# Gated linear attention with a multiplicative FFN on Trainium2: in three early steps the product of q, k and decays moves behind the masks and to the next chunk

## The chip, the cores and the metric

The kernel runs on one core of a Trainium2 chip. The metric is the device time in microseconds (us) of one execution. Below, PE is TensorE (its weight loads are listed as PEld), DVE is VectorE, ACT is ScalarE, POOL is GpSimd, and SP is SyncE, which here only issues DMAs.

## The reference

For 4 batches of 8 heads with 768 positions and a head size of 48, a state of 48 x 48 per head is decayed and added to at each position, and read by the query:

```python
for t in range(S):
    state = alpha[:, :, t, :, None] * state + np.einsum('bhd,bhe->bhde', k[:, :, t], v[:, :, t])
    y[:, :, t] = np.einsum('bhd,bhde->bhe', q[:, :, t], state)
...
a = x @ w1
b = x @ w2
h = a * b @ w3
return (h @ w_out).astype(np.float32)
```

Here x is the attention's output with the heads side by side, 3072 x 384; w1 and w2 are 384 x 1024, w3 is 1024 x 1024 and w_out 1024 x 384. All weights of the FFN come as 64-bit floats, and the attention's inputs as 32-bit floats.

## The kernel before

**Chunks and steps.** Each batch's 768 positions are cut into 6 chunks of 128, so there are N = 24 chunks. The main loop `for n in range(N + 1)` works on several chunks in each of its turns, here called step n: it ends the attention of chunk n-1, makes the scores of chunk n, and prepares the chunks after them. Steps 0 to 5 (n < FIRST = 6) are the early ones, in which the gate weights are also converted. The fourth to sixth step are n=3, 4 and 5.

**One chunk's work.** `load_kq` (L151, L152), `load_a` (L141 for pairs of chunks, L145 for single ones) and `load_v` (L157) issue the loads. `logs` takes the logarithm of alpha on ACT (L316 for a pair, L324 for one chunk). `decays` sums the logarithms along positions with a triangular matmul (L340 for a pair's chunk, L343 or L346 for others) and ACT makes the exponentials of minus and plus the sum (L349, L350) in the tile e. `decayed` multiplies k and q by them on DVE (L359, tile qk). `transposed` turns qk on PE against the identity (L381), and ACT copies the result from two PSUM banks to the tile qkT (L383, two copies). `scores` multiplies q and k on PE (L454; from chunk 8 on L430), and DVE masks the upper triangle with a bitwise and (L457, two instructions; L440 later). `attend_state` multiplies q with the state T (L474), `attend` the masked scores with v (L485; L482 later), and ACT copies the sum to the tile x (L489), which `store` writes to a DRAM tensor xd (L305, SP). `outer` makes the state's next term from qk and v (L393), and DVE adds it to T (L401, L403); a batch's last chunk, n=5, 11 and so on, has no outer product. At every second chunk `advance` multiplies the state with the decays over the chunk on POOL (L410 to L412); these are gathered through DRAM, with small DMAs on POOL's queue (L331, L352, L354 out, L367 back).

**Buffers.** The tile kq has 3 buffers, so the load for chunk n+3 waits until the product of chunk n has read its own. The tile e has 2, qk has 3, qkT 2, the masked scores ms 2, and v 4. All PSUM results use one ring of 8 banks in the order in which the code asks for them.

**Weights.** `to_fp32` converts a 64-bit weight tile in generator steps that `convert` runs: SP loads it raw (L236, 512 KB; up to 4 in flight), ACT converts the low words (L244) and DVE the mantissa (L245) and the exponent (L248); ACT scales the exponent (L249), DVE puts the number together (L251, L252, L253). `load_gates` then splits it: ACT makes the high part (L260), DVE the low one (L262). `third` makes the third part with two matmuls (L276, L277) and a copy on ACT (L278).

**From step 6 on.** `split_early` splits the attention's output, loaded back from xd (L512), into three parts on ACT (L521) and DVE (L522, and L524 twice). From step 7 on pieces of the two gate products (`gate`, matmuls at L554) are run between the attention's parts, the first of them behind the transposes of step 7. After the last chunk come the remaining gate products, the folding of w3 and w_out into one matrix, and the final product, nearly all of it matmuls at L554.

**What sets the order.** The program's own order and its marks set priorities: `after_marks(...)` opens a context in which what is issued stands behind the marked instructions, and a scheduler then orders each engine's queue. Every engine works through its queue in order. SP's DMAs use 8 semaphores in turn, so a DMA waits until the one eight places ahead of it has landed.

Of the kernel before, what the change touches and what calls it, by code (L numbers as in the profile page):

```python
# [48 lines left out]
def kernel(  # L49
# [18 lines left out]
    N = B * NCH  # L68
# [35 lines left out]
    def bank():  # L104
        return ps.tile([C, 512], FP32, tag="bank", name="bank")
# [3 lines left out]
    def after_marks(*names):  # L109
        stack = ExitStack()  # L110
        for x in names:
            stack.enter_context(tc.issue_after(mark[x]))
        return stack
# [22 lines left out]
    def load_a(n):  # L136
        if paired(n):
            if n % 2 == 0:
                b, c = divmod(n, NCH)
                x = pairs[n // 2 % 2]  # L140
                nc.sync.dma_start(out=x.rearrange("p h s d -> p h (s d)"), in_=alpha[b, :, ds(c * C, 2 * C), :].rearrange("h (p s) d -> p h (s d)", s=2))  # L141
                st["a", n] = st["a", n + 1] = x
        elif n < N:
            st["a", n] = inp.tile([C, H, D], FP32, tag="ac", name="ac", bufs=2)
            nc.sync.dma_start(out=st["a", n], in_=rows(alpha, n))  # L145

    def load_kq(n):
        if n >= N:
            return
        st["kq", n] = inp.tile([C, 2, H, D], FP32, tag="kq", name="kq")  # L150
        nc.sync.dma_start(out=st["kq", n][:, 0], in_=rows(k, n))  # L151
        nc.sync.dma_start(out=st["kq", n][:, 1], in_=rows(q, n))  # L152

    def load_v(n):
        if n < N:
            st["v", n] = vs[n % len(vs)]
            (nc.gpsimd if 2 < n < 8 else nc.sync).dma_start(out=st["v", n][:, :, 0:D], in_=rows(v, n))  # L157
# [122 lines left out]
    def fetch(ahead=3):  # L280
        while weights and len(begun) < ahead:
            begun.append(weights.popleft())
            next(begun[-1])

    def convert(steps, ahead=3):

        for _ in range(steps):
            fetch(ahead)
            if not begun:
                return  # L290
            x = begun.popleft()
            try:
                next(x)
                begun.appendleft(x)
            except StopIteration:
                pass
# [4 lines left out]
    def store():  # L301

        while later:
            dst, src = later.popleft()
            nc.sync.dma_start(out=dst, in_=src)  # L305
# [51 lines left out]
    def decayed(n):  # L357
        if n < N:
            mark["qk", n] = nc.vector.tensor_mul(qks[n % 3][:, :, :, 0:D], st.pop(("kq", n)),  # L359
                                 st.pop(("e", n)).rearrange("p i (h d) -> p i h d", h=H)).ins  # L360
# [9 lines left out]
    def transposed(n):  # L370
        if n >= N:
            return
        qk = qks[n % 3]
        qkT = work.tile([C, 2, NP, C], FP32, tag="qkT", name="qkT")

        tp = [bank().rearrange("p (i j c) -> p i j c", i=2, j=NP) for _ in range(2)]
        for i in range(2):
            for j in range(NP):
                for half in range(2):
                    s = ds(DP * half, DP)  # L380
                    nc.tensor.transpose(tp[half][:, i, j, :], qk[s, i, 2 * j:2 * j + 2, :], ident[s, s])  # L381
        for half in range(2):
            mark["qkT", n] = nc.scalar.copy(qkT[:, :, :, ds(DP * half, DP)], tp[half]).ins  # L383
        st["qkT", n] = qkT
# [116 lines left out]
    def load_early(e):  # L501

        first, chunks = EARLY[e]
        if chunks == 3:
            pieces = ((xb[0][:, XB - KM * TG:].bitcast(FP32), 3),)
        else:
            pieces = ((inp.tile([C, 2, H, D], FP32, tag="kq", name="kq").rearrange("p i h d -> p (i h d)"), 2),
                      *((inp.tile([C, H, D], FP32, tag="ac", name="ac", bufs=2).rearrange("p h d -> p (h d)"), 1) for _ in range(2)))
        st["xT", e], at = [], 0
        for x, width in pieces:  # L510
            x = x.rearrange("p (k t) -> p k t", k=KM)
            nc.sync.dma_start(out=x, in_=x_of(first + at, width))  # L512
            st["xT", e].append((x, ds(at * C, width * C)))
            at += width
# [176 lines left out]
    def run(pieces):  # L691

        for _ in range(pieces):
            if not fill:
                return
            try:
                next(fill[0])
            except StopIteration:
                fill.popleft()
# [20 lines left out]


    FIRST = 6
    begin = {FIRST - 3 + 4 * g: (g, range(FH if g < 4 else KF)) for g in range(5)}
    loads = {8: 1, 11: 2, 15: 3, 20: 4}

    for n in range(N + 1):
        if not 1 < n < FIRST:
            store()
        if n in loads:
            load_early(loads[n])  # L730
        if n != 1 and not 2 < n <= FIRST:
            load_a(n + 5)
        raws = (3, 3, 3, 3, 2, 2, 3, 3)[n] if n < 8 else 4
        for m in (n + 3,) * (n <= FIRST) + (n + 4,) * (n >= FIRST):
            load_kq(m)
            if 2 < n <= FIRST and m == n + 3:
                load_a(n + 5)
            if 1 < n < FIRST:
                store()
            if n < FIRST - 2:  # L740
                fetch(raws)
        if n >= FIRST:
            load_v(n + 2)
        if n:
            attend_state(n - 1)
        if n < N:
            scores(n)
        else:
            for j in range(NP):
                for i in range(2):  # L750
                    attend_low(n - 1, j % 2, i, i ^ (j < 2))
        transposed(n + 1)
        if n == 1:
            decays(3)
            load_a(6)
            with after_marks(("e", 3)):
                logs(4)
        if n == FIRST + 1:
            run(2)
        if n < FIRST:  # L760
            with after_marks("pool"):
                load_v(n + 2)
        if n - 2 in begin and n > FIRST:
            g, tiles = begin[n - 2]
            with after_marks(("ms", n), ("qkT", n + 1)):
                split_early(g)
            fill.extend(gate(g, f) for f in tiles)
        if n == FIRST:
            with after_marks("l", ("qkT", n + 1)):
                split_early(0)  # L770
            fill.extend(gate(0, f) for f in begin[n - 3][1])
        pieces = ((3, 3, 2, 0) if n > FIRST + 3 else (0, 3, 3, 0))[(n - FIRST) % 4] if n >= FIRST else 0
        if n == 0:
            with after_marks(("qkT", 0)):
                logs(2)
            decays(2)
            with after_marks(("e", 2)):
                logs(3)
        early, ready = n < FIRST, len(thirds) if n > 2 else n // 2
        marks = (*[("qkT", n + 1)] * (n < N - 1), *[("qk", n + 1), ("ms", n)] * early, *["x3"] * (n - 2 in begin and n > FIRST))  # L780
        if n < N - 2 and n != FIRST:
            with after_marks(*marks):
                convert(2 if early else 1, raws)
        advance(n)
        turn_v(n)
        if n:
            attend(n - 1)
        outer(n)
        if n > FIRST:
            third(ready)  # L790
        run(pieces > 0)
        if early:
            with after_marks(*marks):
                convert(1, raws)
        with after_marks(*[("ms", n)] * (n < 3)):
            decayed(n + 2)
        if not early:
            with after_marks(*[("qkT", n + 1)] * (n < N - 4)):
                logs(n + 4)
        if n == 4:  # L800
            load_early(0)
        convert(early and n > 0, raws)
        run(pieces > 1)
        if n:
            decays(n + 3)
        if n <= FIRST:
            third(ready)
        if 0 < n < FIRST:
            with after_marks(("e", n + 3)):
                logs(n + 4)  # L810
        if n == FIRST:
            with after_marks("x3", ("e", n + 3)):
                convert(2, raws)
        elif n < N - 2:
            convert(n == FIRST - 1 if early else n % 3 == 0, raws)
        if n == FIRST - 1:
            assert len(done) == 2 * KM
        run(pieces > 2)
        if n == N - 3:
            while begun:  # L820
                convert(1)
            weights.extend(load_out(j) for j in range(KF))
            fetch(4)
# [92 lines left out]
```

## Time and profile before

| what | value |
|---|---|
| three runs | 463.62, 464.98 and 462.82 us; median 463.62 |
| the profiled execution | 462.58 us, with a span of 460.8 us from first to last instruction |
| PE busy | 444.3 us (96%) |
| DVE, ACT, POOL busy | 370.1 us (80%), 270.3 us (59%), 85.7 us (19%) |
| PE busy in 20 to 30, 30 to 40, 40 to 50, 50 to 60 us | 8.56, 8.35, 8.59, 9.45 us |
| PE busy in 60 to 80 us | 20.00 us |
| start of the scores (L454) in n=3, 4, 5, 6 | 29.94, 37.07, 44.66, 50.15 us |
| start of the first gate product (L554) | 58.07 us |
| DMA: bytes in all, mean rate | 79.95 MB, 173 GB/s |

Times count from the start of the span. The timeline lists for one engine the start, the length and the name of each instruction, with equal ones merged (x16), and in brackets how long the engine was idle before it and what ended the wait. The list of waits sums these. The DMA view gives for a transfer the time from its issue to its landing. The granted clock of TensorE is 1.00 of full speed in every stretch.

### The profile page before, as it was taken

Reading aid. Unit: us, or ns where it says so; the run is one execution under the profiler, and the core shown is the slowest. Engines: PE = TensorE matmul, PEld = TensorE weight load, DVE = VectorE, ACT = ScalarE, POOL = GpSimd, SP = SyncE. Lnnn points to the kernel's source line nnn. Section 1 sums busy time; section 2 is a strip of 40 time slices with the busy share of each in tenths; the row PEclk is TensorE's granted clock in tenths of the full one; section 3 lists DMA queues with packets and bytes.
Section 4 is the critical chain, followed back from the end, with each engine's and each line's share of the span. In section 5 each row is a group of like instructions: output and inputs, shape, how many; then the busy total and the mean of one; then the engine's idle time right before and its main releaser. Section 6 shows DMA issues by size and latency. Waiting matters only on the chain.

```text
span 460.8 us, 10652 instructions
## 1 busy us (share of the span) xinstructions
PE 444.3 (96%) x4080; PEld 393.4 (85%) x4080; DVE 370.1 (80%) x600; ACT 270.3 (59%) x507; POOL 85.7 (19%) x171
## 2 busy tenths in 40 slices
PE   4987999999999999999999999999999999999996
PEld 2665699898998988888888888888888999999996
DVE  2869997999989989798999899999537566776671
ACT  4775875758668653777975757566436333343430
POOL 6324232315314240012021010100000000000000
PEclk9999999999999999999999999999999999999999
DMA  9999999999998974445966364521119655665511
GB/s 177 259 206 218 266 221 201 243 214 212 188 233 181 242 179 156 155 112 161 301 198 211 116 172 133 177 68 46 48 51 282 203 151 167 187 186 162 155 53 51
DMA packets 149379, 79.95 MB, mean 173 GB/s; under 512 B 97184, under 2 KB 138784, under 8 KB 149328
## 3 DMA queue, kind: packets, MB, share of 16 engines
q1 hardware_dynamic: 143840, 64.84, 57.4%
q0 software_dynamic: 5488, 14.43, 10.5%
q8 instruction: 32, 0.52, 0.5%
q14 instruction: 19, 0.16, 0.1%
HBM read 57.19 MB, written 22.06 MB: 172 GB/s over the span
## 4 chain that ended last, share of the span: by engine, by line
PE 89%; DMA 4%; SPq 2%; DVE 2%; ACT 2%; issue 1%; DVEq 0%; ACTq 0%
PE bank L554 73%; PE bank L430 3%; PE bank L381 3%; PE bank L482 2%; PE bank L474 2%; DMA x<-in_alpha_dram 2%; PE bank L393 1%; DMA kq<-in_q_dram 1%; PE bank L346 1%; PE bank L419 1%; PE bank L343 1%; SPq L305 1%; SPq L145 1%; PE bank L454 1%; PE bank L485 1%
## 5 line engine op out<-in xcount | busy, mean ns | idle before, releaser
L554 PE MATMUL bank<-x,w 128*128 128x512 f32 (+1 forms) x688 | 163.0, 374 | 0.9 <-ACT qkT L383 0.9
L554 PEld LDWEIGHTS bank<-x,w 128*128 128x128 f32 x688 | 124.6, 188 | 21.1 <-ACT qkT L383 1.2
L554 PE MATMUL bank<-w3o,ab 128*128 128x384 f32 x576 | 100.2, 336 | 0.0
L554 PEld LDWEIGHTS bank<-w3o,ab 128*128 128x128 f32 x576 | 99.9, 188 | 0.2
L554 PE MATMUL bank<-x3b,w 128*128 128x512 f32 (+1 forms) x248 | 71.9, 385 | 0.0
L579 ACT ACTIVATE bank<-bank 128x512 f32<-128x512 f32 (+1 forms) x72 | 41.1, 573 | 34.2 <-PE bank L554 34.2
L554 PEld LDWEIGHTS bank<-x3b,w 128*128 128x128 f32 x248 | 46.4, 188 | 8.4
L628 POOL DMA_DIRECT2D abd<-r x33 | 19.3, 584 | 138.0 <-DVE r L614 116.2
L678 DVE TENSOR_TENSOR ab<-abl,ab 128x1024 fp32r<-128x1024 f32 x24 | 29.4, 1224 | 14.4 <-ACT ab L677 14.4
L383 ACT COPY qkT<-bank 128x512 f32<-128x512 f32 x48 | 26.2, 599 | 22.7 <-PE bank L381 22.7
L563 ACT ACTIVATE t<-bank 128x384 f32<-128x384 f32 x24 | 11.8, 493 | 45.9 <-PE bank L554 45.9
L677 ACT ACTIVATE ab<-abl 128x1024 fp32r<-128x1024 f32 x24 | 25.5, 1062 | 22.1 <-PE bank L554 19.8
L554 PE MATMUL bank<-wo,w3T 128*128 128x384 f32 x192 | 36.3, 337 | 0.0
L249 ACT ACTIVATE power<-power,rebias 128x512 uint32<-128x512 uint32 (+1 forms) x36 | 25.3, 702 | 17.2 <-DVE power L248 16.9
L554 PEld LDWEIGHTS bank<-wo,w3T 128*128 128x128 f32 x192 | 34.1, 188 | 1.2
L565 DVE SCALAR_TENSOR_TENSOR o<-bank,t 128x384 f32<-128x384 f32 x24 | 13.4, 558 | 25.9 <-issue 14.3
L359 DVE TENSOR_TENSOR qk<-kq,e 128x768 f32<-128x768 f32 x24 | 22.9, 954 | 13.8 <-ACT e L350 7.8
L614 DVE TENSOR_TENSOR r<-bank,r 128x512 f32<-128x512 f32 x32 | 21.8, 682 | 9.2 <-PE bank L554 7.7
L679 DVE SCALAR_TENSOR_TENSOR ab<-ab,abl 128x1024 fp32r<-128x1024 f32 x24 | 29.2, 1218 | 0.0
L565 DVE SCALAR_TENSOR_TENSOR r<-bank,r 128x384 f32<-128x384 f32 (+1 forms) x40 | 22.8, 576 | 7.4 <-ACT r L563 6.0
L563 ACT ACTIVATE r<-bank 128x384 f32<-128x384 f32 (+1 forms) x40 | 20.8, 526 | 13.1 <-PE bank L554 10.2
L251 DVE SCALAR_TENSOR_TENSOR mant<-mant,raw 128x512 f32<-128x512 uint32 (+1 forms) x36 | 23.4, 650 | 2.2 <-ACT raw L244 2.2
(115 smaller groups left out, 736.9 us busy)
## 6 DMA issues: line engine op xcount, KB each, us to landing
abl<-abd SPq DMA_DIRECT2D x24, 512.0 KB, 4.3
abd<-r POOLq DMA_DIRECT2D x33, 256.0 KB, 3.3
raw<-in_moe_w_dram SPq DMA_DIRECT2D x64, 128.0 KB, 4.0
raw<-in_moe_w_dram SPq DMA_DIRECT2D x12, 512.0 KB, 5.6
kq<-in_k_dram SPq DMA_DIRECT2D x24, 192.0 KB, 5.0
kq<-in_q_dram SPq DMA_DIRECT2D x24, 192.0 KB, 5.5
xd<-x SPq DMA_DIRECT2D x48, 96.0 KB, 4.0
xT<-xd POOLq DMA_DIRECT2D x6, 768.0 KB, 5.4
```

The source lines that it names most:

```text
L249: nc.scalar.activation(power, power, AF.Relu, scale=2.0 ** 23, bias=rebias)
L251: nc.vector.scalar_tensor_tensor(mant, top, 2.0 ** -20, rest, op0=ALU.mult, op1=ALU.add)
L359: mark["qk", n] = nc.vector.tensor_mul(qks[n % 3][:, :, :, 0:D], st.pop(("kq", n)), st.pop(("e", n)).rearrange("p i (h d) -> p i h d", h=H ...
L383: mark["qkT", n] = nc.scalar.copy(qkT[:, :, :, ds(DP * half, DP)], tp[half]).ins
L554: nc.tensor.matmul(p, w[part][i], x[part][i], start=start and part == parts[0] and i == 0, stop=stop and part == parts[-1] and i == n - 1, ...
L563: nc.scalar.activation(t, p1, AF.Copy, scale=(1.0 + 1.0 / P) * scale)
L565: nc.vector.scalar_tensor_tensor(to, p2, scale, t, op0=ALU.mult, op1=ALU.add)
L579: nc.scalar.activation(p, p, AF.Copy, scale=1.0 + 1.0 / P)
L614: nc.vector.tensor_mul(r[0], p, r[0])
L677: nc.scalar.activation(t[:, 0], ab, AF.Copy, scale=1.0 - 2.0 ** -13)
L678: nc.vector.tensor_sub(t[:, 1], ab, t[:, 0].bitcast(FP32))
L679: nc.vector.scalar_tensor_tensor(t[:, 2], t[:, 0].bitcast(FP32), -1.0 - 1.0 / P, ab, op0=ALU.mult, op1=ALU.add)
```

## The change

A tuple SHORT names the steps 3, 4 and 5. In these, `transposed(n + 1)` is no longer called behind the scores but behind the attention's product and `outer`; ahead of it stands `decayed(n + 1)`, the product of q, k and decays of the next chunk, behind the mark of this step's masks. Before, step n made the product of chunk n+2 and used one that the step before had made. The steps 2, 3 and 4 therefore no longer make the product of chunk n+2, and step 5 makes two, that of chunk 6 and, at its old place, that of chunk 7. The weights' conversion, three generator steps at these places, is divided differently: one behind the masks and two behind the product, in place of two and one behind the marks of qkT, qk and ms. The tiles, the buffers and the instructions' number and size stay.

```diff
--- before.py
+++ after.py
@@ -720,6 +720,7 @@
 
 
     FIRST = 6
+    SHORT = (3, 4, 5)
     begin = {FIRST - 3 + 4 * g: (g, range(FH if g < 4 else KF)) for g in range(5)}
     loads = {8: 1, 11: 2, 15: 3, 20: 4}
 
@@ -749,7 +750,8 @@
             for j in range(NP):
                 for i in range(2):
                     attend_low(n - 1, j % 2, i, i ^ (j < 2))
-        transposed(n + 1)
+        if n not in SHORT:
+            transposed(n + 1)
         if n == 1:
             decays(3)
             load_a(6)
@@ -777,8 +779,11 @@
             with after_marks(("e", 2)):
                 logs(3)
         early, ready = n < FIRST, len(thirds) if n > 2 else n // 2
-        marks = (*[("qkT", n + 1)] * (n < N - 1), *[("qk", n + 1), ("ms", n)] * early, *["x3"] * (n - 2 in begin and n > FIRST))
-        if n < N - 2 and n != FIRST:
+        marks = () if n in SHORT else (*[("qkT", n + 1)] * (n < N - 1), *[("qk", n + 1), ("ms", n)] * early, *["x3"] * (n - 2 in begin and n > FIRST))
+        if n in SHORT:
+            with after_marks(("ms", n)):
+                convert(1, raws)
+        elif n < N - 2 and n != FIRST:
             with after_marks(*marks):
                 convert(2 if early else 1, raws)
         advance(n)
@@ -789,11 +794,18 @@
         if n > FIRST:
             third(ready)
         run(pieces > 0)
-        if early:
+        if n in SHORT:
+            with after_marks(("ms", n)):
+                decayed(n + 1)
+            transposed(n + 1)
+            with after_marks(("qk", n + 1)):
+                convert(2, raws)
+        elif early:
             with after_marks(*marks):
                 convert(1, raws)
-        with after_marks(*[("ms", n)] * (n < 3)):
-            decayed(n + 2)
+        if n + 1 not in SHORT:
+            with after_marks(*[("ms", n)] * (n < 3)):
+                decayed(n + 2)
         if not early:
             with after_marks(*[("qkT", n + 1)] * (n < N - 4)):
                 logs(n + 4)
```

## The prediction

> **What bounds the kernel now.** I read the page first, then TensorE's own waits, then the timelines of each engine between 29 us and 62 us, the stretch in which the changed steps run. A step is one turn of the loop over n; the fourth to sixth are n=3, 4 and 5.
>
> ```profile
> span 460.8 us, 10652 instructions
> PE 444.3 (96%) x4080; PEld 393.4 (85%) x4080; DVE 370.1 (80%) x600; ACT 270.3 (59%) x507; POOL 85.7 (19%) x171
> ```
>
> The list of waits of TensorE alone, from 57 us to the end, has one line:
>
> ```profile
> PE bank L554 <- ACT qkT L383: 0.9, 1, 0.9
> ```
>
> So from 57 us on TensorE works without a pause for 400 us. Whatever makes the first gate product (L554) start earlier or later moves the end by as much, and nothing behind it can take it back. TensorE's timeline shows when each step's scores (L454) start and when that product comes:
>
> ```profile
> 29.94 1.16 PE L454 MATMUL bank<-qkT 48*128 48x128 f32 x16
> ...
> 35.81 0.50 PE L276 MATMUL bank<-w,signs 128*128 128x512 f32 x1 [1.25 <-DVE ms L457]
> ...
> 37.07 1.16 PE L454 MATMUL bank<-qkT 48*128 48x128 f32 x16
> ...
> 44.66 1.33 PE L454 MATMUL bank<-qkT 48*128 48x128 f32 x15
> ...
> 50.15 1.16 PE L454 MATMUL bank<-qkT 48*128 48x128 f32 x16
> ...
> 58.07 1.66 PE L554 MATMUL bank<-x,w 128*128 128x384 f32 x8
> ```
>
> First column: start in us; second: length. VectorE's timeline shows why n=3 and n=5 are held: the product (L359) waits for its q and the masks (L457) stand behind it.
>
> ```profile
> 34.20 0.96 DVE L359 TENSOR_TENSOR qk<-kq,e 128x768 f32<-128x768 f32 x1 [2.59 <-DMA kq<-in_q_dram]
> 35.08 1.28 DVE L457 TENSOR_TENSOR ms<-bank,keep 128x512 int32<-128x512 int32 x2
> ...
> 47.35 0.96 DVE L359 TENSOR_TENSOR qk<-kq,e 128x768 f32<-128x768 f32 x1 [0.52 <-DMA kq<-in_q_dram]
> ```
>
> The transfers themselves cannot come sooner: the DMA share is 1.0 or more in each 10 us from 0 to 60 us, and the loads land one behind the other. What ScalarE and SP do with the weights' raw tiles decides the rest:
>
> ```profile
> 32.72 0.41 SPq L236 DMA_DIRECT2D raw<-in_moe_w_dram  x1
> 40.56 0.39 SPq L236 DMA_DIRECT2D raw<-in_moe_w_dram  x1
> ```
> ```profile
> 40.41 1.06 ACT L383 COPY qkT<-bank 128x512 f32<-128x512 f32 x2
> 41.35 0.70 ACT L244 ACTIVATE raw<-raw 128x512 f32<-128x512 uint32 x1
> ```
>
> The DMA view gives 5.1 us to landing for the first of these transfers and 4.6 us for the second: they land at 37.8 and 45.1 us. Today ScalarE converts the first at 41.35, behind the transposed copies of its step, and never waits for it.
>
> **The change part by part.** No instruction is added or removed; the queues of TensorE, VectorE and ScalarE are reordered, and a few DMAs of GpSimd's. The order is that of the built program, whose queues are in order; it isn't what the diff suggests in two places. (a) On ScalarE the early conversion of the next raw tile (L244) now stands before the copies qkT (L383) of n=3 and n=4, not behind them. (b) On VectorE, in n=5 the product of chunk 7 stands ahead of the masks of chunk 5, and that of chunk 6 behind them. SP's order is the same up to its transfers of 76 us, so landings are kept. I now walk through the steps with start-to-start times from the rows: masks 1.2 for both, L262 0.6, L403 0.27, product 0.9, L245 and L248 0.34 each, L251 0.6, L252 and L253 0.7 each; on ScalarE L244 0.57, L249 0.63, both L383 1.0, both L489 0.55, L349 and L350 0.4 each, L260 0.55; on TensorE L474 0.6, L454 1.0, L381 0.65, L485 0.92, L393 0.55, L340 1.5, L343 0.9, L276 with L277 0.67.
>
> n=3. Scores end at 31.1, masks run from 31.55 (VectorE is busy till then) instead of 35.08: the wait for kq of chunk 5 is gone. L262, L403 and the product of chunk 4 follow to 34.55. TensorE has done L485 and L393 by 32.45, and waits 2.1 us; transposes 34.6 to 35.3, L340 and L276 to 37.4.
> n=4. L474 ends at 38.0; scores need qkT of chunk 4. ScalarE: L260, L316, L244, two L489 to 34.1, then L244 on the raw tile that lands at 37.8; L249; copies 39.1 to 40.1. Scores start at 40.2, not 37.07: **+3.1**. Queued behind ScalarE's wait are the copies and both exponentials of chunk 6, and TensorE waits for the copies. Masks 41.4 to 42.6, L262 to 43.2; L403 needs T of GpSimd's L412, which today ends at 44.01 because its decays land at 40.9; so L403 at 44.05, product of chunk 5 to 45.3, transposes 45.35, L340, L276 to 48.1.
> n=5. L474, then scores at 48.7, not 44.66: **+4.0** (the raw tile of 45.1 is in time here: L244 to 45.7, L489, L249, copies to 47.9). The product of chunk 7 needs the exponentials of L340's result (L349 47.8, L260 after L253 at 48.4, L350 to 49.5): 49.5 to 50.4; masks to 51.65, L262 to 52.2, product of chunk 6 to 53.15. TensorE has only L485 to do (no L393 in this step) and waits from 50.65 to 53.2. Then L381, L343, L276 to 55.4.
> n=6. L474; copies 54.5 to 55.6 behind an L249 that needs L248 at 53.85; scores at 56.05, not 50.15: **+5.9**. From here TensorE alone sets the pace: L381, L485, L393, L343, two thirds, scores and transposes of n=7, 6.9 us against 7.9 today (0.54 us of waiting at L381 goes): L554 at 62.95. The split it needs is ready: L521 58.7, L522 to 61.3, L524 to 62.6; its input landed at 54.5.
>
> Sum: 62.95 - 58.07 = **+4.9 us**, that is 3.1 + 0.9 + 1.9 - 1.0. Other moves cost nothing: GpSimd now waits for alpha of chunk 10 before it stores the last row of chunk 8's decays, T of chunk 8 then comes about 3.5 us later (67.1 to some 70.5), and is read first by L403, today at 71.96 and then 4.9 later; SP's alpha of chunk 11 goes 2.3 us later (L324 frees its buffer) and its reader 4.9 us later.
>
> The wait for raw tiles ahead of L383 is not in the trace of before. Its bounds: landing took 4.6 us to 8.0 us for raw tiles from 24 us to 41 us, so -0.5 to +2.9 on the first term; I take the 5.1 us of the very same transfer. The second term is 0 if T is ready early, the third between 0 and 2.
>
> TensorE now has gaps of 2.1 to 2.7 us, where the longest after 10 us was 1.25. In the rows the two L343 took 1.62 us at 4.44, after 4.4 us of idling, and 0.91 at 48.15: a slow state exists, though the granted clock shows 1.00 in both. After the gap of 1.25 the L276 took its usual 0.50.
>
> **The rivals.**
> Faster masks win (not slower). If the raw tile had landed by 34.1, when ScalarE gets to it, n=3 to n=5 would keep only what the change frees. The gain ends at the split: its input lands at 54.5, L521 and L522 take 1.2 and 1.3, so L554 can start at 57.0, 1.05 earlier: 462.6 us. For it: 4.66 us of TensorE's idling lie between 29 and 52 us. Against it: the landing at 37.8 is 3.7 us too late. 8 in 100.
> The later steps catch up. The second and third term overlap with other waits and vanish: 3.1 - 1.0 = +2.1, 465.7 us. Against it: T's time and the order on VectorE are fixed. 10 in 100.
> TensorE slows after the gaps. The path behind the gaps of n=4 and n=5 has 4.4 and 3.9 us of TensorE's work; at 1.62/0.91 it would be 0.78 times 8.3 = 6.5 us longer: 475 us. 7 in 100, as 1.25 us did nothing. The Trainium skill, TensorE: Matmul & The Clock Gate, Part 1, says the array's clock halves after an idle window of about 3.4 us and recovers after a busy one; by that rule no gap here reaches it and this rival is void, and the slow first rows agree with it.
>
> **How the numbers follow.** The sum is made on the profiled execution, 462.58 us (span 460.8, 1.8 around it), which gives 467.5; the median of the three runs, 463.62, is 1.0 above it, and I put the sum on the median: 463.6 + 4.9 = 468.5 us, with 75 in 100. Its own bounds are 467.2 to 470.8: late landings move the top by up to 2.9 us, of which 0.9 hides in the wait for T; early ones and smaller later terms move the bottom. The range takes in the catch-up case: 465.7 to 470.8. About 0.5% (2.3 us) is what a measurement here can tell from no change: within it lie 462.6 and most of 465.7, 13 in 100; slower 85; faster 2.
>
> **What would show it.** In the changed profile: ScalarE idle before an L244 until a raw tile at about 37.8; L454 at about 40.2, 48.7 and 56.0; the masks of n=3 at 31.5; TensorE idle before L381 for 2 us and more in n=3, 4 and 5, released by the product; L359 of chunk 7 ahead of the masks of n=5; L554 at about 63; TensorE's busy time still 444. It is wrong if the first raw conversion does not wait, if the first L554 starts before 61, or if TensorE pauses after it.

## The result, and the profile after

The changed kernel takes 469.77 us (median of 6 runs, 468.05 to 471.62) beside 463.37 us for the kernel before (6 runs): a ratio of 1.0149, with an interval of 1.0128 to 1.017. Measured twice more, the ratio was 1.0119 (1.0081 to 1.0158) and 1.0107 (1.0081 to 1.0134). By the medians the change costs 5.4 to 6.4 us, where 4.9 was forecast; all three medians (469.77, 470.09, 469.53 us) lie in the range of 465.7 to 470.8, above its point of 468.5. Two runs far above the others of their kernel, 2449 us in the experiment act_mark and 468.75 us in marks_only, are left out of the medians and ratios below. The profiled execution took 468.05 us with a span of 466.3.

Three lines of the page after: the span, the engines' busy time, and the row of TensorE's granted clock in 40 slices, in tenths of full speed.

```profile
span 466.3 us, 10650 instructions
PE 447.6 (96%) x4080; PEld 396.8 (85%) x4080; DVE 371.5 (80%) x600; ACT 271.1 (58%) x507; POOL 88.1 (19%) x171
...
PEclk9998899999999999999999999999999999999999
```

The same 4080 matmuls are busy for 3.3 us more, and the fourth and fifth slice (35 to 58 us) no longer show a full clock. TensorE's own waits from 57 us to the end are again a single line:

```profile
PE bank L554 <- ACT qkT L383: 1.2, 1, 1.2
```

So nearly all was lost before the first gate product, as in the reading of before. TensorE's timeline, the scores (L454), the transposes (L381) and that product (L554):

```profile
30.12 1.16 PE L454 MATMUL bank<-qkT 48*128 48x128 f32 x16
34.48 0.81 PE L381 MATMUL bank<-ident,qk 64*128 64x64 f32 x16 [1.72 <-DVE qk L359]
39.48 1.82 PE L454 MATMUL bank<-qkT 48*128 48x128 f32 x16 [1.64 <-ACT qkT L383]
45.21 0.81 PE L381 MATMUL bank<-ident,qk 64*128 64x64 f32 x16 [1.50 <-DVE qk L359]
50.09 1.16 PE L454 MATMUL bank<-qkT 48*128 48x128 f32 x16
54.19 0.71 PE L381 MATMUL bank<-ident,qk 64*128 64x64 f32 x16 [1.91 <-DVE qk L359]
56.73 1.16 PE L454 MATMUL bank<-qkT 48*128 48x128 f32 x16
...
63.16 1.66 PE L554 MATMUL bank<-x,w 128*128 128x384 f32 x8
```

The brackets show the new waits: three times TensorE stands ahead of its transposes for the product, and once ahead of the scores of n=4 for the copies qkT. One length is odd: the scores of n=4 take 1.82 us where all others take 1.16. L554 starts at 63.16 instead of 58.07, 5.1 us later, and the span is 5.5 us longer. VectorE and ScalarE, the lines that answer to those of before:

```profile
31.31 1.29 DVE L457 TENSOR_TENSOR ms<-bank,keep 128x512 int32<-128x512 int32 x2 [0.38 <-PE bank L454]
...
43.84 0.36 DVE L403 TENSOR_TENSOR T<-bank,T 128x192 f32<-128x192 f32 x1 [0.59 <-PE bank L393]
...
49.77 0.96 DVE L359 TENSOR_TENSOR qk<-kq,e 128x768 f32<-128x768 f32 x1 [1.82 <-ACT e L350]
51.29 1.29 DVE L457 TENSOR_TENSOR ms<-bank,keep 128x512 int32<-128x512 int32 x2 [0.56 <-PE bank L454]
```
```profile
37.18 0.68 ACT L244 ACTIVATE raw<-raw 128x512 f32<-128x512 uint32 x1 [3.75 <-DMA raw<-in_moe_w_dram]
38.37 1.05 ACT L383 COPY qkT<-bank 128x512 f32<-128x512 f32 x2
44.10 0.67 ACT L244 ACTIVATE raw<-raw 128x512 f32<-128x512 uint32 x1 [2.67 <-DMA raw<-in_moe_w_dram]
```

The masks of n=3 start at 31.31 (35.08 before): the wait for q is gone, as the change means it to be. ScalarE now idles 3.75 us for the raw tile that lands at 37.2, with the copies queued behind it. In n=5 the masks stand behind the product of chunk 7, but what ended their wait is the scores' bank: they would have started no earlier without that product.

The oddity is the clock. The table of stretches of 3.41 us, cut where the granted clock changes, with TensorE's busy time and the granted clock behind it (then the DMA share and GB/s):

```profile
36.39:39.80 3.41, 1.77 (x24) 1.00 1.17 171
39.80:43.21 3.41, 3.41 (x38) 0.50 1.18 306
43.21:46.62 3.41, 1.91 (x34) 1.00 1.24 195
46.62:50.03 3.41, 3.41 (x21) 0.50 0.86 178
50.03:53.45 3.42, 2.25 (x36) 1.00 0.99 241
```

After a stretch in which TensorE was busy for 1.77 of 3.41 us, it works at half clock for the whole next one; after a busy one it is at full clock again; then the same once more. In the profile of the kernel before the clock was full from 12.65 us, where its record begins, to the last microsecond.

### The profile page after: what moved, and what is told of

It reads as the page before. It is cut to its first block, busy times and chain, and to the rows that moved or that the text cites. A ratio compares the mean times of both kernels' runs of the same rounds, so it can differ in the third digit from the quotient of the medians.

```text
span 466.3 us, 10650 instructions
## 1 busy us (share of the span) xinstructions
PE 447.6 (96%) x4080; PEld 396.8 (85%) x4080; DVE 371.5 (80%) x600; ACT 271.1 (58%) x507; POOL 88.1 (19%) x171
## 4 chain that ended last, share of the span: by engine, by line
PE 93%; DMA 2%; DVE 2%; ACT 1%; issue 1%; SPq 0%; DVEq 0%; ACTq 0%
PE bank L554 72%; PE bank L381 3%; PE bank L430 3%; PE bank L474 2%; PE bank L454 2%; PE bank L340 2%; PE bank L482 2%; DMA raw<-in_moe_w_dram 2%; PE bank L393 2%; PE bank L485 1%; PE bank L346 1%; PE bank L343 1%; PE bank L419 1%; DVE qk L359 1%; DMA ac<-in_alpha_dram 1%
## 5 line engine op out<-in xcount | busy, mean ns | idle before, releaser
L554 PE MATMUL bank<-x,w 128*128 128x512 f32 (+1 forms) x688 | 163.1, 375 | 1.2 <-ACT qkT L383 1.2
L554 PEld LDWEIGHTS bank<-x,w 128*128 128x128 f32 x688 | 124.8, 188 | 21.4 <-ACT qkT L383 1.5
L554 PE MATMUL bank<-w3o,ab 128*128 128x384 f32 x576 | 100.2, 336 | 0.0
L554 PEld LDWEIGHTS bank<-w3o,ab 128*128 128x128 f32 x576 | 99.9, 188 | 0.2
L554 PE MATMUL bank<-x3b,w 128*128 128x512 f32 (+1 forms) x248 | 71.9, 385 | 0.0
L554 PEld LDWEIGHTS bank<-x3b,w 128*128 128x128 f32 x248 | 46.4, 188 | 8.4 <-issue 0.2
L554 PE MATMUL bank<-wo,w3T 128*128 128x384 f32 x192 | 36.3, 337 | 0.0
L554 PEld LDWEIGHTS bank<-wo,w3T 128*128 128x128 f32 x192 | 34.1, 188 | 1.2
L244 ACT ACTIVATE raw<-raw 128x512 f32<-128x512 uint32 (+1 forms) x36 | 23.2, 651 | 6.4 <-DMA raw<-in_moe_w_dram 6.4
```

The source lines that it names most:

```text
L244: nc.scalar.activation(rest, low, AF.Copy, scale=2.0 ** -52)
L554: nc.tensor.matmul(p, w[part][i], x[part][i], start=start and part == parts[0] and i == 0, stop=stop and part == parts[-1] and i == n - 1, ...
```

## The experiments

Two questions were open. **How much do the new waits cost, and which?** Theory A: they take each other's place (raw tile, T, scores), so undoing one gives nothing; what holds is that the next chunk's product stands behind the masks and behind L403, and TensorE idles through that chain. The rival, the forecast's own reading: each named wait is a term, and undoing it gives the term back. **What does the half clock cost?** Theory A: it follows the idling and costs the rest; the rival: it falls where TensorE waits anyway.

**act_mark: conversion behind the copies again.**

```diff
             transposed(n + 1)
-            with after_marks(("qk", n + 1)):
+            with after_marks(("qk", n + 1), ("qkT", n + 1)):
                 convert(2, raws)
```

> The changed kernel with the two conversion steps of n=3 to 5 queued behind the copies qkT on ScalarE as well, so that no raw tile is waited for ahead of them. Theory A (waits take each other's place: without it the product of chunk 5 still stands behind the state's sum L403, which waits for GpSimd's T at 43.7 us): the scores of n=4 start at 38.0 instead of 39.5, those of n=5 still at about 48.5, the first gate product at 62 to 63; 5 to 6 us over before. Theory B (the wait for the raw tile is a loss by itself): the scores of all later steps and the end come about 3 us earlier, 3 us over before.

Measured: 468.36 us, ratio 1.0099 (1.0066 to 1.0132). TensorE's timeline, and VectorE's L403:

```profile
37.11 1.16 PE L454 MATMUL bank<-qkT 48*128 48x128 f32 x16
44.62 1.21 PE L381 MATMUL bank<-ident,qk 64*128 64x64 f32 x16 [4.87 <-DVE qk L359]
50.52 1.16 PE L454 MATMUL bank<-qkT 48*128 48x128 f32 x16
```
```profile
43.26 0.36 DVE L403 TENSOR_TENSOR T<-bank,T 128x192 f32<-128x192 f32 x1 [3.06 <-POOL T L412]
```

The scores of n=4 come at 37.11, as before the change: the first term is undone in full. But the product of chunk 5 stands behind L403, which waits for GpSimd's T until 43.26, so TensorE now idles 4.87 us ahead of L381 instead of 1.50, the clock falls to half for two stretches (43.6 to 50.4 us), and the scores of n=5 (50.52, where about 48.5 was expected) and L554 (63.58) are no earlier. One wait took the other's place: the transposes start 1.36 us behind L403 here (43.26 to 44.62) and 1.37 us behind it in the changed kernel (43.84 to 45.21), whenever the copies came.

**dve_mark: the product of chunk 7 behind that of chunk 6.**

```diff
         if n + 1 not in SHORT:
-            with after_marks(*[("ms", n)] * (n < 3)):
+            with after_marks(*[("ms", n)] * (n < 3), *[("qk", n + 1)] * (n in SHORT)):
                 decayed(n + 2)
```

> The changed kernel with the product of chunk 7 queued behind that of chunk 6 in n=5, and so behind the masks. Theory A (in the changed kernel's trace the masks of n=5 wait 0.56 us for TensorE's scores after that product has ended): no change beyond 0.5 us against the changed kernel, 6 us over before. Theory B (as the prediction's third term has it, the order of the products costs 1.9 us): 4.5 us over before.

Measured: 468.36 us, 1.0103 (1.0069 to 1.0137); L554 at 63.07. The masks of n=5 are now first on VectorE, and nothing is gained: as the line of 51.29 above shows, they wait for the scores. L554 alone would not show it, since the second stretch at half clock falls later in this profile (53.58 to 56.99 us, behind the scores of n=5 at 48.45); but the transposes of n=5 follow these scores by 4.10 us in both (48.45 to 52.55, and 50.09 to 54.19).

**qk_first: both marks, and the product ahead of L403.** The outer product and its addition L403 are queued behind the product.

```diff
-        outer(n)
+        if n in SHORT:
+            with after_marks(("ms", n)):
+                decayed(n + 1)
+            with after_marks(("qk", n + 1)):
+                outer(n)
+        else:
+            outer(n)
```

> The changed kernel with both marks (conversion behind qkT on ScalarE, product of chunk 7 behind that of chunk 6) and, in n=3 to 5, the state's sum L403 queued behind the product. Theory A (with the raw tile, T is what holds the changed kernel): product of chunk 5 at 41 us, scores of n=5 at 45.5 and of n=6 at 52, first gate product at 59, 1 to 1.5 us over before. Theory B (the loop from scores over masks, product, transposes and copies within one step is too long by itself): scores of n=6 at 54 and later, 3 us and more over before.

Measured: 466.96 us, 1.0076 (1.0049 to 1.0104). TensorE, and ScalarE much later:

```profile
42.46 0.80 PE L381 MATMUL bank<-ident,qk 64*128 64x64 f32 x16 [1.46 <-DVE qk L359]
45.74 1.16 PE L454 MATMUL bank<-qkT 48*128 48x128 f32 x16
...
58.83 1.66 PE L554 MATMUL bank<-x,w 128*128 128x384 f32 x8
```
```profile
134.33 0.49 ACT L563 ACTIVATE r<-bank 128x384 f32<-128x384 f32 x1 [5.62 <-DMA abd<-r]
```

This undoes most of the loss ahead of L554: 58.83, 0.8 us behind the kernel before, with the clock at 1.00 up to there. The two marks alone left L554 at 63.58 and 63.07, so the place of the product behind L403 and T was the largest single part, the clock's share that came with it included. The time is 3.5 us over before, where 1 to 1.5 were expected: in the profiled execution a store of r landed late, ScalarE waited for its buffer, TensorE for ScalarE (3.49 us), and two stretches at half clock followed. SP's order behind 76 us is another one in this kernel, so the late wait is not the start's doing alone. Its runs scatter from 465.48 to 469.43.

**step3_only: the change in the fourth step alone.**

```diff
-    SHORT = (3, 4, 5)
+    SHORT = (3,)
```

together with the marks of act_mark and dve_mark.

> The changed kernel with SHORT = (3,): only the fourth step makes its next chunk's product behind the masks; the product of chunk 5 follows it, and the weights' conversion stands behind both marks, qk and qkT. Theory A (the change costs its time in n=4 and n=5, where the product of the next chunk stands behind the addition L403 and this behind T, while n=3 pays only with TensorE's idling): masks of n=3 at about 31.5 us, a gap of about 2 us ahead of L381 in n=3, scores of n=4 at 37 to 38 us, of n=5 at 44.3 to 45 us, where T sets them as before, first L554 at 57.5 to 58.5 us, and the time within 0.5 us of the kernel before plus what one phase at half clock costs (up to 1.7 us). Theory B (each of the three steps costs about a third): the first L554 at 59.5 us or later, and the time 1.5 to 2.5 us above the kernel before.

Measured: 464.17 us, 1.0004 (0.9983 to 1.0025).

L554 starts at 58.58. The fourth step has the gap of 1.72 us ahead of L381 as the changed kernel has it, and its scores of n=4 come at 38.39, a little later than expected; it costs nothing, since in n=4 TensorE waits for T anyway (scores of n=5 at 44.67, before 44.66). So in this form, where the copies do not wait for the raw tile, the fourth step is free, and the loss is that of n=4 and n=5.

**marks_only: the conversion ahead of the copies, and nothing else.** The kernel before with one condition.

```diff
-        marks = (*[("qkT", n + 1)] * (n < N - 1), ...
+        marks = (*[("qkT", n + 1)] * (n < N - 1 and not 2 < n < FIRST), ...
```

> The kernel before with one side effect of the change alone: the weights' conversion of steps 3, 4 and 5 has no mark on the qkT of the next chunk, so that ScalarE converts a raw tile ahead of the copies L383; the products, masks and transposes stay where they were. Theory A (the wait for the raw tile costs only because the change also moves the transposes behind the attention, where the copies have no slack): first L554 within 0.5 us of 58.07, and the time within 0.5 us of the kernel before. Theory B (the conversion ahead of the copies costs 2 to 3 us by itself, as the first term of the forecast reads): scores of n=4 or n=5 2 us or more later than before, and the time 1.5 us or more above.

Measured: 463.96 us, 0.9993 (0.9968 to 1.0018).

```profile
37.09 0.70 ACT L244 ACTIVATE raw<-raw 128x512 f32<-128x512 uint32 x1 [1.51 <-DMA raw<-in_moe_w_dram]
40.41 1.05 ACT L383 COPY qkT<-bank 128x512 f32<-128x512 f32 x2
```

ScalarE waits for the same raw tile, 3.3 us ahead of copies that come at 40.41 as before: free. The wait for the raw tile costs only where the transposes have moved behind the attention.

**masks_first and masks_first_t: is there a gain in the masks at all?** In both, only the masks stand ahead of the product; the product is still that of the chunk after the next. The second also queues a load of v on GpSimd behind T.

```diff
-        with after_marks(*[("ms", n)] * (n < 3)):
+        with after_marks(*[("ms", n)] * (n < FIRST)):
             decayed(n + 2)
```

> The kernel before with one part alone: the masks of steps 3, 4 and 5 stand ahead of the product on VectorE; the product is still that of the chunk after the next, and the transposes and the weights' conversion stay where they were. Theory A (in the kernel before, the masks' wait behind the product holds TensorE for about 1 us in n=3, but the state T sets step 5 and the landing of the split's input at 54.5 us the end): the gap of 1.25 us ahead of L276 in n=3 goes, L554 starts at 57.0 to 57.6 instead of 58.07, and the time is 0.4 to 1.0 us below the kernel before. Theory B (the waits take each other's place here too): L554 at 58 or later, and the time within 0.4 us of the kernel before or above it.

> The run masks_first, and in n=4 the load of v for chunk 6 stands behind the state's last addition (L412) on GpSimd, so that T is there about 1.2 us earlier, at about 42.8 us. Theory A (the end is bounded by the split's input): scores of n=5 come about 1 us earlier than in masks_first, but L554 not before 57.0, and the time is within 0.3 us of masks_first. Theory B (T is what sets the end): L554 comes 1 us or more ahead of masks_first, and the time is about 1.0 to 2.0 us below the kernel before.

Measured: 464.24 us, 1.0009 (0.9989 to 1.003), and 464.79 us, 1.0011 (0.9987 to 1.0036). In masks_first L554 starts at 57.30, as theory A had it, but the 0.4 to 1.0 us that it expected of the time do not show: within what can be measured it is that of before. In masks_first_t T is there at 42.2 and the scores of n=5 start at 42.86, 1.5 us earlier than in masks_first (44.35). Then VectorE shows where it goes:

```profile
52.09 0.96 DVE L359 TENSOR_TENSOR qk<-kq,e 128x768 f32<-128x768 f32 x1 [3.02 <-DMA kq<-in_q_dram]
```

The next chunk's q lands at 52.1, the masks of n=6 stand behind its product, TensorE waits 2.94 us, runs at half clock for two stretches from 55.1 on, and L554 comes at 59.09. The time is that of masks_first, as expected, but what bounds it is another transfer than the split's input, which theory A had named, and L554 is 2 us later than that bound.

**spin, spin6 and spin5: filling TensorE's gaps.** The changed kernel with 14, 6 and 5 matmuls of the identity with itself ahead of the transposes of the three steps (spin and spin6 also ahead of the scores of n=4). The lines of spin5:

```diff
         outer(n)
+        if n in (3, 4, 5):
+            spin = bank()[:, 0:C]
+            for _ in range(5):
+                nc.tensor.matmul(spin, ident, ident, start=True, stop=True)
```

> The changed kernel with 14 products of the identity with itself (some 1.7 us) put into each of the four gaps of TensorE: ahead of the transposes in n=3, 4 and 5 and ahead of the scores of n=4. Their result is read by nobody. Theory A (idling makes the array slow: granted clock 0.5 at 39.8 to 43.2 and 46.6 to 50.0): granted clock 1.00 throughout, L454 of n=4 back at 1.1 us and L340 of n=4 at 1.5 us, the first gate product 1 to 2 us earlier, runs closer together, 4 to 5 us over before. Theory B (the slow phases have another cause): the slow phases stay, and the time is that of the changed kernel, 6.4 us over before, or longer.

> The changed kernel with 6 matmuls of the identity with itself in TensorE's gaps ahead of the masked product (L485) and the transposes (L381); by the 14 that took 3.39 us they take about 1.45 us each time, a little less than the gaps of 1.5 to 1.9 us. The outputs are the same. Theory A (the change costs about 3.5 us by its waits, and the idling makes the clock fall to half, which costs the rest): the granted clock stays at 1.00 from 17 us on, the first L554 comes at 61 to 62 us, and the time is 3 to 5 us above the kernel before, 1 to 2 us below the changed kernel of this call. Theory B (the slow clock comes from something else, or falls where nothing waits): phases of 0.5 remain or L554 stays at 63 or later, and the time is that of the changed kernel or more.

> The changed kernel with 5 matmuls of the identity with itself ahead of the transposes of steps 3, 4 and 5, some 1.3 us each time by the 1.60 us that six took; the order of every other instruction on all engines and queues is the changed kernel's own, which was not so in the run spin6. The outputs are the same. Theory A (the idling costs clock, and the clock costs time): fewer or no phases of 0.5 between 30 and 60 us, the first L554 at 61 to 62.5 us, TensorE waiting no more than 1.5 us behind it, and the time 1 to 2 us below the changed kernel of this call. Theory B (the phases at half clock fall where TensorE waits anyway, or other waits behind 57 us take the gain back): the time is within 0.5 us of the changed kernel of this call, or above.

> The changed kernel itself once more, on the chip that the next three runs use. Both theories expect what was measured: 4.5 to 6.5 us above the kernel before, the first gate product (L554) at about 63 us, and phases of half clock between 39 and 57 us.

> The changed kernel itself, for comparison with spin5 on the same chip. Both theories expect 4.5 to 6.5 us above the kernel before.

spin: 471.31 us, 1.0151 (1.0099 to 1.0202); the clock is 1.00 from 16.5 us on, but the fill was too long for its gaps, twice what had been reckoned:

```profile
32.95 3.39 PE L801 MATMUL bank<-ident 128*128 128x128 f32 x28
```

It settles the cause of the half clock (all four runs have a mean clock of 0.999 or 1.000, where the changed kernel's 16 have 0.981 to 0.995) and nothing on the time.

spin6: 469.88 us, 1.0125 (1.0088 to 1.0163), beside 470.09 for the changed kernel measured with it (after_again). The clock is 1.00 from 17.3 us on and L554 starts at 61.56, where after_again has 64.58; yet the time is the same. Against the kernel before its parts of the attention are 3.5 us late at 81 us and 6.1 us at 119 us; between them ScalarE idles 3.44 us for the landing of a store of r. The added matmuls had also changed the order of SP's queue from about 44 us on, so this run could not say whether the clock costs time.

spin5 has every queue in the changed kernel's own order but for the fill. 467.89 us, 1.0079 (1.0054 to 1.0104), beside 469.53 us, 1.0107 (1.0081 to 1.0134), for the changed kernel measured with it (after_third): 1.6 us less, between the 1 and 2 us expected, though the intervals overlap. The stretches of after_third's profile, and then of spin5's:

```profile
35.98:39.39 3.41, 1.52 (x20) 1.00 1.16 186
39.40:42.81 3.41, 3.29 (x28) 0.50 1.15 292
42.81:46.22 3.41, 1.92 (x30) 0.50 1.23 203
46.23:49.63 3.40, 3.40 (x20) 0.50 0.97 194
```
```profile
36.39:39.80 3.41, 2.90 (x33) 1.00 1.21 196
39.80:43.21 3.41, 2.71 (x49) 1.00 1.10 286
43.21:46.62 3.41, 2.50 (x28) 1.00 1.26 201
```

With the fill TensorE is busy for 2.50 us and more of each of these stretches, and in this profile the clock doesn't fall. This fill doesn't suffice in every run: three of the six have a mean clock of 1.000, the others 0.992, 0.992 and 0.995. With six matmuls all four runs are at 0.996 to 1.000. L554 starts at 62.00 in spin5 and at 67.16 in after_third, whose clock was half for five stretches. Behind L554 spin5 gives some of that back: TensorE waits 2.6 us there, more than the 1.5 expected.

## Why the prediction was right in sign and range, and where it was not

The forecast was slower by 4.9 us, all of it ahead of L554 and none given back. That the end follows L554 held: from L554 to the end the kernel before takes 402.7 us (460.8 - 58.07) and the changed one 403.1 (466.3 - 63.16). It holds no closer than 2 us, though: in the other profiles, spin6 and qk_first aside, this way takes 402.5 to 404.7 us. The times of L454 and L554, as forecast and as the profiles have them; the last column is spin5, the waits without the half clock:

| start of | before | forecast | after | after_third | spin5 |
|---|---|---|---|---|---|
| scores n=3 | 29.94 | as before | 30.12 | 29.40 | 31.28 |
| scores n=4 | 37.07 | 40.2 | 39.48 | 39.52 | 40.50 |
| scores n=5 | 44.66 | 48.7 | 50.09 | 50.82 | 48.55 |
| scores n=6 | 50.15 | 56.05 | 56.73 | 58.59 | 55.57 |
| first L554 | 58.07 | 62.95 | 63.16 | 67.16 | 62.00 |

The near hit of 62.95 and 63.16 is a sum of errors of both signs. Taken from step to step, which leaves out that executions start the scores of n=3 up to 1.9 us apart:

| term (over before) | forecast | after | spin5 |
|---|---|---|---|
| n=3 to n=4 | +3.1 | +2.2 | +2.1 |
| n=4 to n=5 | +0.9 | +3.0 | +0.5 |
| n=5 to n=6 | +1.9 | +1.2 | +1.5 |
| n=6 to L554 | -1.0 | -1.5 | -1.5 |
| sum | +4.9 | +4.9 | +2.6 |

**First term.** The mechanism is in the trace: ScalarE idles at L244 until the raw tile lands, at 37.2 instead of 37.8, copies behind it, scores at 39.48. It was 0.9 too large, 0.6 of it that landing. But it was no term of its own: act_mark took the wait away and gained nothing at L554, as T held the next step instead, and marks_only had the wait without any cost. In the forecast's own walk T at 44.05 sets the scores of n=5 whatever the copies do, so that its 3.1 and 0.9 are one term of 4.0, set by T.

**Second term.** What the forecast says of T held: L403 starts at 43.84 (44.05 forecast), the product ends at 45.07 (45.3), the transposes start at 45.21 (45.35). In the profile after the bracket of L403 names TensorE's L393, which ended at 43.72, at half clock; but T was there only at 43.61, so the first stretch at half clock cost about 0.1 us. In spin5 T is what ends the wait:

```profile
43.99 0.36 DVE L403 TENSOR_TENSOR T<-bank,T 128x192 f32<-128x192 f32 x1 [0.39 <-POOL T L412]
```

What the forecast lacks comes behind the transposes. From them to the scores of n=5 it reckons 3.35 us; spin5, at full clock, takes 3.19, and the changed kernel 4.88, as its stretch from 46.62 to 50.03 ran at half clock. So of the 2.1 us by which the second term is too small, about 1.4 is the clock (50.09 against 48.7), and 0.7 stands against the scores of n=4 that came 0.7 earlier than forecast.

**Third term.** Its size was about right and its cause mostly wrong. The forecast held the masks of n=5 to be late because the product of chunk 7 stands ahead of them; in the profile after they wait for the scores, and dve_mark, which turns the order, gains nothing. In spin5, where the scores come earlier, the masks do stand behind that product, but by 0.3 us only (they start 1.50 us behind the scores instead of 1.20). What is left is the gap of 1.9 us ahead of L381: masks, conversion and product come one behind the other, and TensorE has only L485 to do in this step. qk_first shows the weight of the chain in n=4: with the product ahead of L403 the scores of n=5 come at 45.74 and L554 at 58.83.

**Fourth term.** The way from the scores of n=6 to L554 takes 6.43 us instead of the 6.9 reckoned. The top of the range is not quite its own sum: 468.5 + 2.9 - 0.9 is 470.5, not 470.8; all three medians lie below either.

**The step that failed** is the rival "TensorE slows after the gaps", put at 7 in 100 and at nothing in the sum. No gap reached 3.4 us, so it was held to be void, and the gap of 1.25 us in the kernel before, after which L276 had its usual length, was taken as evidence. The full clock that the forecast read beside the slow first L343 was no reading either, as the record of the clock begins at 12.65 us there. The runs showed half clock in every profile of the changed kernel, in two to five stretches of 3.41 us. The gap is not what counts: gaps of 1.5 to 2.6 us were enough, with other idle time in the same stretch (the three ahead of L381 are 1.72, 1.50 and 1.91 us in the profile after, below the 2 us and more that were named). In that profile the stretches ahead of the two falls had TensorE busy for 1.77 and 1.91 us of 3.41. The cost was below the 6.5 us named there. Over the 16 runs of the changed kernel the span grows as the mean clock falls, from 465.9 us at 0.995 to 469.7 at 0.982 and 469.9 at 0.981. One stretch of 3.41 us at half clock lowers the mean by 0.0036 (3.41 x 0.5 / 468); a straight line through the 16 gives 0.9 us of span for each such stretch and covers three quarters of the variance. At 1.00, three runs of spin5 have spans of 464.6, 465.3 and 466.7 us. By this, as an estimate, the waits cost about 2.6 to 3.8 us (the sum above; spin5's median over before, 467.89 - 464.08), not 4.9, and the clock the rest of the 5.4 to 6.4. That the forecast came so near is luck in part: it put the waits too high and the clock at nothing.

The Trainium skill, TensorE: Matmul & The Clock Gate, Part 1, gives half clock "after ≥1 idle window (~3.4µs)". The length of the stretches agrees with these traces; that the window must be idle does not, as 1.91 of 3.41 us were busy. The same page's section A second HAM failure mode: psum-queue depth-cycling tells of a kernel whose frequent short idling made the clock swing; the prediction weighed only the first rule, and this second one is what the traces here bear out.

**The other rivals.** "Faster masks win" was priced at 462.6 us. masks_first is its purest form: L554 came 0.8 us earlier (57.30) and the time stayed within 0.3% of before; masks_first_t pulled the scores of n=5 forward by another 1.5 us and met the landing of the next q. The kernel before works so close to its transfers in these steps that a wait removed there has little to give. "The later steps catch up" (465.7) didn't happen, though the waits did overlap. The moves on GpSimd and SP cost nothing that shows: TensorE's only wait behind 57 us in the profile after is 1.2 us for copies (0.9 before). That nothing behind 57 us takes the delay back holds for the changed kernel; it isn't a law, as spin6 and qk_first lost 4 and 6 us more there than the kernel before, with late stores of r among the causes. TensorE's busy time, said to stay at 444, is 447.6, the half clock's doing.

**What stays open.** Why masks_first with L554 0.8 us earlier shows no shorter time. Its profile, at full clock, has 1.9 us of waits behind 57 us where before has 0.9. Its other runs are at half clock more often: 7 of 12 have a mean clock of 0.993 or less, beside 9 of 23 of the kernel before measured with it. Whether that takes the gain wasn't tried. How busy a stretch must be to keep the clock can be narrowed down, not settled. Cut on the grid on which the clock changes, the 14 profiles have 19 stretches at full clock with TensorE busy for 1.52 us of 3.41 or less, and half clock follows each of them (11 stand at the program's end); of 18 with 1.75 to 2.25 us it follows four (1.77, 1.91, 1.92 and 2.25, while another with 1.92 is followed by full clock); with 2.26 us or more it never does. What decides between 1.75 and 2.25 us is not known. Whether the rest of the difference between qk_first's start (0.8 us late) and its time (ratio 1.0076, about 3.5 us) lies in half clock or in SP's other order wasn't told apart; five of its ten runs have a mean clock of 0.993.

## What to carry to other kernels

A wait removed from one engine is a gain only up to the next thing that is late there: list for each step all that the bounding engine needs, with times, and take the latest, rather than adding up waits; here undoing either of two of them (act_mark, dve_mark) gave nothing. When an order of work leaves the matmul engine with several pauses of 1.5 to 2 us in a row, count the clock as well: sum its busy time over stretches of 3.4 us, and where that is below half, or not far above it, allow about 1 us more for each such stretch, as it was in this kernel. A mark that ties work of one engine to an instruction of another is lost when the mark is replaced; read the built order on every engine, and test each difference alone.

## What the runs showed of the hardware that was not expected

TensorE's granted clock went from 1.00 to 0.50 for whole stretches of 3.41 us after stretches in which it was partly busy (1.77 and 1.91 us of 3.41 in one profile, 1.52 in another), and matmuls in them took longer (scores 1.82 to 2.08 us instead of 1.16). It came back after one stretch in most cases; twice it stayed at half for a second one although TensorE had been busy for all 3.41 us of the first (56.47 to 59.88 us in after_third, 55.09 to 58.50 in masks_first_t). Matmuls in the idle time kept the clock up, the more of them the surer: 14 per gap in all four runs, 5 per gap in three of six. Such a matmul of 128x128 with 128 columns in 32-bit floats is listed as two and took about 0.24 us in a dense row (14 in 3.39 us). How many stretches fall differs from run to run of the same program, by the mean clock from about one to five here, and goes with most of the scatter of the changed kernel (465.9 to 469.9 us of span). The kernel before has such runs too: 12 of its 63 runs beside the experiments have a mean clock of 0.991 to 0.993.
